# Another deal of three elementwise steps: who rounds and who subtracts the activated sums between two matmuls

## The chip, the cores and the metric

The kernel runs on one core of one Trainium2 chip. A core has five engines, each with its own in-order queue: TensorE (PE; its weight loads are listed apart as PEld), VectorE (DVE), ScalarE (ACT), GpSimd (POOL) and SyncE (SP, which here only issues DMAs). An instruction that waits for a semaphore holds up everything behind it on its own engine. The metric is the device time of one launch in microseconds (us), lower is better; it is given as the median of three runs, and one further execution was taken with the hardware profiler.

## The reference, cut to what matters

Eight batches of eight heads of causal attention (576 positions, head size 64), mixed with a retrieval from a small memory matrix, give a token matrix x of 4608 rows by 512 columns. A feed-forward network follows:

```python
def _moe_ref(x, w_in, w_out):          # x: 4608 x 512
    h = x @ w_in                       # 512 x 2048
    g = h * (1.0 / (1.0 + np.exp(-h))) # h * sigmoid(h)
    return (g @ w_out).astype(np.float32)
```

The kernel writes h * sigmoid(h) as 0.5 * h * (1 + tanh(h / 2)) and applies the 0.5 to the output. To keep the accuracy of 32 bits out of matmuls that round their operands, every operand is held as an upper part (the value rounded to the type `fp32r`) and a lower part (the value less its upper part), and each product is three matmuls: upper by upper, upper by lower, lower by upper.

## The kernel before, in words

Two generators are interleaved. `attention` goes through the 64 heads: one iteration computes the scores of one head and the values of the head before it. `ffn` goes through 18 units of 256 tokens. A unit is 8 steps p; each step makes two 128-row chunks of h in one PSUM bank (24 matmuls, L552), activates them, and multiplies the activated sums g by two chunks of `w_out` into the unit's output banks `acc` (12 matmuls, L532). In the program's text the multiplication of step p-1 stands between the matmuls of step p and the activation of step p, so that PE has work while the activation of a step is under way.

The activation of a step is a chain over three engines: tanh on ScalarE out of PSUM (L563, into the tile `th`), `(th + 1) * h` on VectorE (L564, into `th` again; h is read from PSUM, and when this is done the bank of h is free), the rounding of `th` to the upper part `hi` of the tile `g` on GpSimd (L567), and the subtraction `th - hi` into the lower part `lo` of `g` on VectorE (L568). The matmuls of L532 read `hi` in the first two of each three and `lo` in the third. While attention runs, h has one PSUM bank (`ps_h`); after the last head, odd steps take banks of `ps_t` too. `th` has 4 buffers (tag "row", shared with the output tile), `g` has 4.

The other users of the same engines, as far as the prediction speaks of them: on VectorE the masked scores (L252), the small statistics of a softmax row (`st`: L284 to L302; L290 and L299 read two SBUF tensors), the normaliser (`nrm`: L330 to L333) and the lower parts `pl` and `qp` (L407, L359); on ScalarE the exponentials (L254, L294), and the upper parts `ph` (L406) and `kk`, `qq` (L230, L231, L233); on GpSimd the scaling of the probabilities (L304, five instructions a head, released by L302), the lower parts `kk`, `ql` (L232, L235) and `vs` (L316). L161 and L162 split the weights in the first 200 us: L161 rounds on ScalarE, L162 subtracts on GpSimd, with tiles of the same 128x512 shape as `g`.

The loop at the end of the kernel (L589) decides how many steps of `ffn` follow each step of `attention` (`FFN_RATE`, `FIRST_RATE`). The order of the instructions on each engine is then not the program's: the tile framework is told to schedule with planned costs (`schedule_with_timeline_sim=True`, L631) and moves instructions within what the dependences and buffers allow. A change of engine or operation in one place therefore moves others too.

Of the kernel before, what the change touches and what calls it, by code (L numbers as in the profile page):

```python
# [13 lines left out]
ALU = mybir.AluOpType  # L14
# [26 lines left out]
def memory_attention_then_silu_ffn(ctx, tc, q, k, v, M_prev, z_prev, beta, w_in, w_out, out):  # L41
    nc = tc.nc
# [30 lines left out]
    def f(ap):  # L73
        return ap.bitcast(F32)
# [11 lines left out]
        out=mask[:, 3 * P:], in_=mask[:, 3 * P:], pattern=[[-1, P]], base=0, channel_multiplier=1,  # L86
# [392 lines left out]
    def flow():  # L479
        if flow_order:  # L480
            while flow_order[0] not in ready:
                yield "prepare"
            x = flow_order.pop(0)
            t = weight_tile(*x)
            nc.sync.dma_start(out=f(t), in_=scratch[x])
            flowing.append((x, t))

    def fetch(kind, c):
        if (kind, c) not in FLOW:
            return weight[kind, c]  # L490
        x, t = flowing.pop(0)
        assert x == (kind, c)
        return t

    def split_x(u):
        xu = []
        for kk in range(KD):
            t = pool.tile([P, 2, T], F32R, tag="xu", name="xu", bufs=XU_BUFS)
            t0 = u * T
            while t0 < (u + 1) * T:  # L500
                b = t0 // S
                n = min((b + 1) * S, (u + 1) * T) - t0
                src, o = xt[b, kk][:, t0 - b * S:t0 - b * S + n], t0 - u * T
                nc.scalar.copy(t[:, 0, o:o + n], src)
                nc.vector.tensor_tensor(out=t[:, 1, o:o + n], in0=src, in1=f(t[:, 0, o:o + n]), op=ALU.subtract)  # L505
                t0 += n
            xu.append(t)
        return xu

    def heads_needed(u):  # L510
        return ((u + 1) * T - 1) // S * H + H

    def ffn():
        ahead = None
        for _ in range(FLOW_BUFS):
            yield from flow()
        for u in range(NU):
            while done[0] < heads_needed(u):
                yield "wait"
            xu = ahead or split_x(u)  # L520
            ahead = None
            bank, tag = (ps_s, "s") if done[0] == B * H and u % 2 else (ps_a, "a")
            acc = [bank.tile([P, DM], F32, tag=tag, name="acc") for _ in range(T // P)]

            def second(p, g):
                for c in range(2):
                    w = fetch("o", 2 * p + c)
                    for t in range(T // P):
                        at = slice(t * P, (t + 1) * P)
                        terms = [(g[:, gi, c, at], w[:, wi]) for gi, wi in ((0, 0), (0, 1), (1, 0))]  # L530
                        for n, (ta, tb) in enumerate(terms):
                            nc.tensor.matmul(  # L532
                                acc[t], ta, tb, start=p == 0 and c == 0 and n == 0,
                                stop=p == NP - 1 and c == 1 and n == len(terms) - 1)
                    if ("o", 2 * p + c) in FLOW:
                        yield from flow()

            before = None
            for p in range(NP):
                while not {("i", 2 * p), ("i", 2 * p + 1)} <= ready:  # L540
                    yield "prepare"
                if done[0] == B * H and p % 2:
                    h = ps_t.tile([P, 2, T], F32, tag="t", name="h")
                else:
                    h = ps_h.tile([P, 2, T], F32, tag="h", name="h")
                for c in range(2):
                    w = fetch("i", 2 * p + c)
                    w4 = w.rearrange("p a (k f) -> p a k f", f=P)
                    for kk in range(KD):
                        terms = [(w4[:, wi, kk], xu[kk][:, xi]) for wi, xi in ((0, 0), (0, 1), (1, 0))]  # L550
                        for n, (ta, tb) in enumerate(terms):
                            nc.tensor.matmul(  # L552
                                h[:, c], ta, tb, start=kk == 0 and n == 0,
                                stop=kk == KD - 1 and n == len(terms) - 1)
                    if ("i", 2 * p + c) in FLOW:
                        yield from flow()
                yield
                if before:
                    yield from second(*before)

                h = h.rearrange("p c t -> p (c t)")
                th = pool.tile([P, 2 * T], F32, tag="row", name="th", bufs=ROW_BUFS)
                nc.scalar.activation(th, h, AF.Tanh, scale=0.5)  # L563
                nc.vector.scalar_tensor_tensor(out=th, in0=th, scalar=1.0, in1=h, op0=ALU.add, op1=ALU.mult)  # L564
                g = pool.tile([P, 2, 2, T], F32R, tag="g", name="g", bufs=G_BUFS)
                hi, lo = (g[:, j].rearrange("p c t -> p (c t)") for j in range(2))
                nc.gpsimd.tensor_scalar(hi, th, 1.0, 1.0, op0=ALU.mult, op1=ALU.mult)  # L567
                nc.vector.tensor_tensor(out=lo, in0=th, in1=f(hi), op=ALU.subtract)  # L568
                while not {("o", 2 * p), ("o", 2 * p + 1)} <= ready:
                    yield "prepare"  # L570
                before = p, g
                if p == NP - 2 and u + 1 < NU and done[0] >= heads_needed(u + 1):
                    ahead = split_x(u + 1)
                yield
            yield from second(*before)
            for t in range(T // P):
                o = pool.tile([P, DM], F32, tag="row", name="o", bufs=ROW_BUFS)
                nc.scalar.activation(o, acc[t], AF.Copy, scale=0.5)
                r0 = u * T + t * P
                nc.sync.dma_start(out=out[r0:r0 + P, :], in_=o)  # L580
            yield

    A_STEPS, F_STEPS = 9, 2 * NP + 1
    att, prep, prod = attention(), preparation(), ffn()
    steps, produced, steps_made = 0, 0.0, 0
    going = True
# [46 lines left out]
```

## Time and profile before

| what | value |
|---|---|
| three runs, median (lowest to highest) | 1333.85 us (1330.49 to 1334.98) |
| the profiled execution, its own time / span of its instructions | 1331.87 us / 1330.1 us |
| mean granted TensorE clock | 0.978 |
| busy share of the span | PE 95%, PEld 82%, DVE 72%, ACT 61%, POOL 60% |
| of the chain that ended last | PE 71%, DVE 13%, ACT 6%, DMA 4%, issue 3%, POOL 2% |

In the profile a row names the line of the kernel, the engine, the operation, the tile written and the tiles read, the shape and the count; then busy time in us, the mean ns of one, and the idle time of the engine ahead of it with what ended that idle time. In rows of one tile or one line the three durations are the smallest, the median and the largest. The program has three stages: until about 178 us only attention and the splitting of the weights run, from there to about 1120 us attention and the feed-forward network run together, and from 1120 us to the end only the feed-forward network is left. The first instruction that the change concerns starts at 178.7 us.

### The profile page before, as it was taken

The page shows a single profiled execution, that of the slowest core. Times are in us where ns is not written, and L with a number is a line of the kernel's source. Part 1 is how long each engine was busy: PE and PEld are TensorE (multiplying, and loading weights), DVE is VectorE, ACT ScalarE, POOL GpSimd, SP SyncE. Part 2 cuts the span into 40 slices and gives each one's busy share as a digit, 9 for nine tenths or more (in the row PEclk, how much of TensorE's full clock was granted, in tenths as well). Part 3 has the DMA queues.
Part 4 walks back from the last instruction along what each step waited for, and adds up shares of the span by engine and source line. Part 5 has one row for each costly group of instructions (what it writes and reads, how often), then busy time and mean ns, then how long its engine had stood idle before and what let it go on. Part 6 is the DMA issues. An engine that isn't in the chain of part 4 may idle for free.

```text
span 1330.1 us, 24649 instructions
## 1 busy us (share of the span) xinstructions
PE 1269.9 (95%) x7858; PEld 1084.7 (82%) x7858; DVE 963.4 (72%) x2580; ACT 805.2 (61%) x1999; POOL 798.1 (60%) x1169
## 2 busy tenths in 40 slices
PE   6988989999999999999999999999999999999998
PEld 2343458898989899899989898989898889899997
DVE  7988985788888878877888787778878875322222
ACT  6777765667676767667776676666767663111111
POOL 6888994676666667766677665656576653101110
PEclk9986799999999999999999999999999999999999
DMA  6766555554555545555555455455545432444444
GB/s 163 191 177 176 151 152 159 136 140 134 135 150 137 151 116 135 152 137 151 136 149 140 136 139 136 131 149 136 137 134 145 128 101 80 155 137 155 156 159 143
DMA packets 302994, 190.39 MB, mean 143 GB/s; under 512 B 258832, under 2 KB 267024, under 8 KB 302864
## 3 DMA queue, kind: packets, MB, share of 16 engines
q1 hardware_dynamic: 302864, 188.82, 50.8%
q8 instruction: 62, 1.02, 0.3%
q14 instruction: 68, 0.56, 0.1%
HBM read 173.02 MB, written 15.73 MB: 142 GB/s over the span
## 4 chain that ended last, share of the span: by engine, by line
PE 71%; DVE 13%; ACT 6%; DMA 4%; issue 3%; POOL 2%; SPq 1%; DVEq 0%; POOLq 0%; ACTq 0%
PE h L552 27%; PE acc L532 24%; PE x L422 7%; PE s L250 5%; PE tp L376 4%; DVE s L252 2%; PE x L414 1%; PE tq L351 1%; DMA zb<-in_z_prev 1%; DVE xu L505 1%; DMA flow<-wo_s 1%; DVE th L564 1%; DVE wy L152 1%; DVE wy L159 1%; ACT p L254 1%
## 5 line engine op out<-in xcount | busy, mean ns | idle before, releaser
L552 PE MATMUL h<-xu,wi 128*128 128x256 f32 x2592 | 373.8, 287 | 10.0 <-DVE th L564 7.3
L552 PEld LDWEIGHTS h<-xu,wi 128*128 128x128 f32 x2592 | 342.6, 191 | 24.9 <-DVE th L564 5.9
L304 POOL TENSOR_SCALAR p<-p,st 128x384 f32<-128x384 f32 (+3 forms) x320 | 186.1, 600 | 127.4 <-DVE st L302 121.2
L532 PE MATMUL acc<-wo,g 128*128 128x512 f32 x864 | 244.8, 399 | 0.0
L567 POOL TENSOR_SCALAR g<-th 128x512 fp32r<-128x512 f32 x144 | 90.9, 631 | 236.8 <-DVE th L564 205.7
L532 PE MATMUL acc<-flow,g 128*128 128x512 f32 x864 | 230.9, 395 | 0.7 <-DMA flow<-wo_s 0.7
L254 ACT ACTIVATE p<-s,st 128x128 f32<-128x128 f32 (+3 forms) x256 | 134.9, 528 | 123.2 <-DVE st L252 93.7
L564 DVE SCALAR_TENSOR_TENSOR th<-th,h 128x512 f32<-128x512 f32 x144 | 98.5, 685 | 130.5 <-ACT th L563 128.0
L532 PEld LDWEIGHTS acc<-flow,g 128*128 128x128 f32 x864 | 158.9, 188 | 33.9 <-DMA flow<-wo_s 1.8
L532 PEld LDWEIGHTS acc<-wo,g 128*128 128x128 f32 x864 | 150.0, 189 | 20.1 <-POOL p L304 0.5
L563 ACT ACTIVATE th<-h 128x512 f32<-128x512 f32 x144 | 85.6, 595 | 128.1 <-PE h L552 127.3
L407 DVE TENSOR_TENSOR pl<-tp,ph 128x384 fp32r<-128x384 f32 x216 | 118.4, 550 | 38.1 <-ACT ph L406 33.9
L568 DVE TENSOR_TENSOR g<-th,g 128x512 fp32r<-128x512 f32 x144 | 104.8, 728 | 50.5 <-POOL g L567 49.3
L252 DVE CUSTOM_DVE_ANT_0 s<-s,mask 128x128 f32<-128x128 f32 (+3 forms) x256 | 125.4, 492 | 11.5 <-PE s L250 6.7
L376 PE MATMUL tp<-ident,p 128*128 128x128 f32 x640 | 123.0, 292 | 8.5 <-DVE qp L359 3.7
L552 PE MATMUL h<-xu,flow 128*128 128x256 f32 x864 | 126.7, 284 | 0.0
L406 ACT CAST ph<-tp 128x384 fp32r<-128x384 f32 x216 | 104.7, 490 | 23.6 <-PE x L422 14.7
L552 PEld LDWEIGHTS h<-xu,flow 128*128 128x128 f32 x864 | 114.1, 190 | 0.9 <-issue 0.3
L376 PEld LDWEIGHTS tp<-ident,p 128*128 128x128 f32 x640 | 81.5, 147 | 37.4 <-POOL p L304 9.3
L235 POOL TENSOR_TENSOR ql<-tt,qq 64x512 fp32r<-64x512 f32 x54 | 73.2, 1356 | 20.6 <-ACT qq L231 11.3
L328 POOL TENSOR_TENSOR r<-e,zb 128x320 f32<-128x320 f32 x64 | 59.8, 935 | 42.4 <-DVE e L327 35.4
L422 PE MATMUL x<-pl,vs 128*128 128x256 f32 x324 | 81.7, 307 | 0.0
(103 smaller groups left out, 2430.2 us busy)
## 6 DMA issues: line engine op xcount, KB each, us to landing
flow<-wo_s SPq DMA_DIRECT2D x144, 512.0 KB, 3.5
flow<-wi_s SPq DMA_DIRECT2D x72, 512.0 KB, 3.8
raw<-in_k SPq DMA_DIRECT2D x128, 72.0 KB, 2.3
raw<-in_q SPq DMA_DIRECT2D x128, 72.0 KB, 2.5
out<-o SPq DMA_DIRECT2D x36, 256.0 KB, 4.2
wraw<-in_moe_w_in SPq DMA_DIRECT2D x16, 512.0 KB, 4.4
qn<-in_q SPq DMA_DIRECT2D x64, 128.0 KB, 2.9
vr<-in_v SPq DMA_DIRECT2D x64, 128.0 KB, 2.6
```

What stands on the lines that cost most here:

```text
L252: anchor["dve"] = nc.vector.tensor_tensor_reduce(s, s, mask[:, 3 * P - P * i:], QS, 3.0e38, ALU.add, ALU.min, st[:, i:i + 1]).ins
L254: nc.scalar.activation(pt, s, AF.Exp, bias=st[:, i:i + 1], scale=-1.0, accum_out=st[:, 10 + i:11 + i])
L304: nc.gpsimd.tensor_scalar(pb[x], pb[x], st[:, 15 + x:16 + x], 1.0, op0=ALU.mult, op1=ALU.mult)
L376: nc.tensor.transpose(t[:, o:o + P], pb[i][:, P * j:P * j + P], ident)
L406: nc.scalar.copy(ph[:, 0:o], t[:, 0:o])
L407: nc.vector.tensor_tensor(out=pl[:, 0:cut], in0=t[:, 0:cut], in1=f(ph[:, 0:cut]), op=ALU.subtract)
L422: nc.tensor.matmul(x[0:rows, q0:n], vs[0:n_k, j], part[0:n_k, o:o + n - q0], start=False, stop=last)
L532: nc.tensor.matmul(acc[t], ta, tb, start=p == 0 and c == 0 and n == 0, stop=p == NP - 1 and c == 1 and n == len(terms) - 1)
L552: nc.tensor.matmul(h[:, c], ta, tb, start=kk == 0 and n == 0, stop=kk == KD - 1 and n == len(terms) - 1)
L564: nc.vector.scalar_tensor_tensor(out=th, in0=th, scalar=1.0, in1=h, op0=ALU.add, op1=ALU.mult)
L567: nc.gpsimd.tensor_scalar(hi, th, 1.0, 1.0, op0=ALU.mult, op1=ALU.mult)
L568: nc.vector.tensor_tensor(out=lo, in0=th, in1=f(hi), op=ALU.subtract)
```

## The change

The product of tanh and h stays on VectorE. The rounding to `hi` goes from GpSimd (a multiplication by 1.0 twice) to ScalarE (a copy), and the subtraction for `lo` goes from VectorE to GpSimd. Line numbers do not shift.

```diff
                 nc.vector.scalar_tensor_tensor(out=th, in0=th, scalar=1.0, in1=h, op0=ALU.add, op1=ALU.mult)
                 g = pool.tile([P, 2, 2, T], F32R, tag="g", name="g", bufs=G_BUFS)
                 hi, lo = (g[:, j].rearrange("p c t -> p (c t)") for j in range(2))
-                nc.gpsimd.tensor_scalar(hi, th, 1.0, 1.0, op0=ALU.mult, op1=ALU.mult)
-                nc.vector.tensor_tensor(out=lo, in0=th, in1=f(hi), op=ALU.subtract)
+                nc.scalar.copy(hi, th)
+                nc.gpsimd.tensor_tensor(out=lo, in0=th, in1=f(hi), op=ALU.subtract)
                 while not {("o", 2 * p), ("o", 2 * p + 1)} <= ready:
                     yield "prepare"
```

The order on all engines is the same up to the first step of the feed-forward network, and differs from there on. Three places show how.

On ScalarE, about the middle of the kernel (a tanh and what follows it, among the work of the heads with the tiles `qq_150` and `qq_151`), before:

```order
L275 COPY pair<-s 64x256
L231 CAST qq_151<-tt 64x576
L233 CAST qq_151<-tt 64x576
L563 ACTIVATE th<-h 128x512
L358 CAST qp<-tq 64x2x128
L275 COPY pair<-s 64x320
L230 CAST kk<-tt 64x576
L237 CAST qq_151<-qq_151 128x64
L326 ACTIVATE r<-qn_147 128x320
```

and with the change:

```order
L563 ACTIVATE th<-h 128x512
L275 COPY pair<-s 64x256
L231 CAST qq_151<-tt 64x576
L233 CAST qq_151<-tt 64x576
L358 CAST qp<-tq 64x2x128
L326 ACTIVATE r<-qn_147 128x320
L567 CAST g<-th 128x512
L275 COPY pair<-s 64x320
L230 CAST kk<-tt 64x576
```

The copy (L567) stands five rows behind its tanh here, and the tanh itself moved ahead of the copies of `pair` and `qq`. Over all 144 steps the copy stands directly behind its tanh or with up to seven rows between.

On GpSimd, at the same head, from the end of one head's scaling of the probabilities on, before:

```order
L307 COPY p_6214<-p_6214 64x64
L235 TENSOR_TENSOR ql_154<-tt,qq_150 64x512
L235 TENSOR_TENSOR qq_150<-tt,qq_150 64x64
L318 TENSOR_SCALAR ms<-mr 128x64
L567 TENSOR_SCALAR g<-th 128x512
L319 TENSOR_TENSOR ms<-mr,ms 128x64
L277 TENSOR_TENSOR pair<-pair,mask 64x64
L328 TENSOR_TENSOR r<-e,zb 128x320
```

and with the change:

```order
L307 COPY p_6214<-p_6214 64x64
L318 TENSOR_SCALAR ms<-mr 128x64
L319 TENSOR_TENSOR ms<-mr,ms 128x64
L568 TENSOR_TENSOR g<-th,g 128x512
L328 TENSOR_TENSOR r<-e,zb 128x320
L235 TENSOR_TENSOR ql_154<-tt,qq_150 64x512
L235 TENSOR_TENSOR qq_150<-tt,qq_150 64x64
L277 TENSOR_TENSOR pair<-pair,mask 64x64
```

The subtraction stands where the rounding stood, give or take a few rows, and `ql` has gone behind it.

On PE, the last rows of the program (the matmuls of the last steps; `wo_142` and `wo_144` are the first of the two `w_out` chunks of the last two steps, `flow` is a chunk that is fetched anew), before:

```order
L532 MATMUL acc<-wo_142,g 128x512 x4
L552 MATMUL h<-xu,flow 128x256 x12
L532 MATMUL acc<-wo_142,g 128x512 x2
L532 MATMUL acc<-flow,g 128x512 x6
L532 MATMUL acc<-wo_144,g 128x512 x6
L532 MATMUL acc<-flow,g 128x512 x6
```

and with the change:

```order
L532 MATMUL acc<-wo_142,g 128x512 x6
L552 MATMUL h<-xu,flow 128x256 x12
L532 MATMUL acc<-flow,g 128x512 x6
L532 MATMUL acc<-wo_144,g 128x512 x6
L532 MATMUL acc<-flow,g 128x512 x6
```

Between the last matmul of h and the first that reads the last `g`, eight matmuls stood before, and six stand now.

## The prediction

> **What bounds the kernel now.** I read the busy time by stage first, then PE's own waits in the long middle stage, then the instructions of the tiles `th` and `g`. The first row holds the stage in which attention and the feed-forward network run together, the second the stage with the network alone (columns: stretch, its length, busy us and count of each engine, granted clock, DMA share, GB/s).
>
> ```profile
> 250.00:1120.00 870.00, 847.02 (x5702) 775.04 (x5701) 702.48 (x1993) 596.02 (x1505) 577.97 (x914) 1.00 0.50 136
> 1120.00:1330.00 210.00, 205.35 (x1306) 185.80 (x1304) 58.47 (x98) 34.09 (x69) 23.86 (x37) 1.00 0.44 146
> ```
>
> PE is busy for 847.02 of 870 us (97%) at the full clock, and for 205.35 of the last 210. VectorE is the next at 81%, ScalarE has 69%, GpSimd 66%. The change takes nothing from PE, so in the middle it can touch only the 870 - 847 = 23 us in which PE stands, and these PE names completely:
>
> ```profile
> PE h L552 <- DVE th L564: 6.5, 10, 1.6
> PE tp L376 <- DVE qp L359: 3.7, 2, 2.9
> PE s L250 <- ACT p L254: 3.6, 4, 2.3
> PE s L250 <- DVE st L284: 2.0, 2, 1.0
> PE s L274 <- ACT p L254: 1.8, 2, 1.2
> PE tp L376 <- DVE pl L407: 1.5, 4, 0.5
> PE x L422 <- ACT ph L406: 1.1, 2, 0.5
> PE x L414 <- DVE xt L430: 0.8, 1, 0.8
> PE tq L351 <- DVE ph L410: 0.7, 1, 0.7
> PE h L552 <- DVE st L290: 0.5, 1, 0.5
> PE tq L351 <- ACT th L563: 0.2, 1, 0.2
> PE acc L532 <- DMA flow<-wo_s: 0.2, 1, 0.2
> ```
>
> (Who waited, for whom, us in total, times, longest.) VectorE ends 15.7 us of these waits, ScalarE 6.7, GpSimd none. The largest, 6.5 us, is the one bank of h, which is free when L564 has read it. No matmul of `acc` waits for `g`: neither L567 nor L568 sets PE's time today. What the two cost is room on their engines. VectorE is also whom the others wait for:
>
> ```profile
> ACT p L254 <- DVE st L252: 83.8, 87, 3.0
> ACT p L294 <- DVE st L291: 47.3, 34, 3.2
> POOL p L304 <- DVE st L302: 115.5, 46, 6.4
> POOL g L567 <- DVE th L564: 23.8, 21, 3.4
> DVE g L568 <- POOL g L567: 22.4, 25, 1.8
> ```
>
> **The change part by part, in the middle stage.** It holds 100 of the 144 steps. Their durations, and those of the nearest rows for the two new instructions (the splitting of the weights, the same shape and types, on the engines to which the work goes):
>
> ```profile
> L567 POOL TENSOR_SCALAR g<-th x100: 611/622/729, 257.4 to 1113.6; 128x512 fp32r<-128x512 f32 x100
> L568 DVE TENSOR_TENSOR g<-th,g x100: 645/692/1356, 258.1 to 1114.3; 128x512 fp32r<-128x512 f32 x100
> L564 DVE SCALAR_TENSOR_TENSOR th<-th,h x101: 648/687/691, 256.7 to 1119.6; 128x512 f32<-128x512 f32 x101
> L161 ACT CAST wi<-wy x12: 601/618/652, 12.6 to 155.5; 128x512 fp32r<-128x512 f32 x12
> L162 POOL TENSOR_TENSOR wi<-wy,wi x12: 1264/1278/1725, 13.3 to 161.5; 128x512 fp32r<-128x512 f32 x12
> L568 DVE TENSOR_TENSOR g<-th,g 128x512 fp32r<-128x512 f32 x100 | 72.6, 726 | 23.4 <-POOL g L567 22.4
> ```
>
> *VectorE* loses 72.6 us of work, and the 22.4 us for which it stood in front of L568 for the rounding. Its load goes from 702 to 630 us of 870.
>
> *ScalarE* gains 100 x 0.618 = 62 us: 596 to 658. It also gains a wait that GpSimd had: for L564. GpSimd stood 23.8 us for it in 21 of the 100 steps. With the order shown, from no to seven rows stand between tanh and copy. I bound this idle time by 0 and by one L564 of 0.687 us a step, 69 us, and take 25, by the row of the wait that it replaces. Behind the copy on ScalarE stand the exponentials and the upper parts that PE's transposes and value matmuls need.
>
> *GpSimd* loses 100 x 0.622 = 62 us and gains 100 x 1.278 = 128, or 173 if every one took the longest, 1.725: 578 to 644 us, at most 689. No work of GpSimd is waited for by PE in the list above. The load of the three helpers becomes 73%, 76% and 74%, where the fullest was at 81%.
>
> Not all of VectorE's 95 us stay free. Its small operations with two SBUF inputs are slow against a copy of the same size:
>
> ```profile
> L290 DVE TENSOR_TENSOR st<-st 64x1 f32<-64x1 f32 x102 | 32.0, 313 | 1.1
> L331 DVE SCALAR_TENSOR_TENSOR nrm<-nrm,over 128x5 f32<-128x5 f32 x50 | 25.6, 511 | 1.1
> L299 DVE SCALAR_TENSOR_TENSOR st<-st,over 128x5 f32<-128x5 f32 x52 | 10.2, 196 | 1.1
> L289 DVE COPY st<-st 64x1 f32<-64x1 f32 x102 | 15.2, 149 | 7.2 <-ACT p L294 3.9
> L290 DVE TENSOR_TENSOR st<-st x128: 107/151/1387, 20.4 to 1109.1; 64x1 f32<-64x1 f32 x128
> ```
>
> Over the 149 ns of the copy they lose (313 - 149) x 102 + (511 - 149) x 50 + (196 - 149) x 52 ns = 37 us, and a subtraction of one column that took 1387 ns lasted about as long as a GpSimd subtraction. If they stand behind whatever GpSimd runs, the loss grows with its share and the square of the lengths: a step's 0.62 squared (0.39) becomes 1.28 squared (1.63), two steps a head, against about 9 us squared a head for the rest of GpSimd's work (an estimate from its rows). That is a quarter more, +9 us on VectorE, +37 at the most if the loss doubled. Even then VectorE ends below its load of before.
>
> The Trainium skill, "SBUF — State Buffer", section "Who interferes with whom", states it as a lock: a VectorE instruction with two SBUF inputs and a GpSimd instruction that reads SBUF exclude each other for the whole instruction. The 1387 ns row agrees. The rule speaks against longer GpSimd subtractions, and for taking L568 off VectorE, since L568 itself reads two SBUF tensors; L564 reads one and is not held (its largest duration is 691 ns, its median 687). By that rule at its hardest, the loss doubled to +37 us, VectorE would stand at 77%, its idle time would grow by a fifth and not a third, and the sum at the end would be +1.6 us (1335.5) instead of the one below.
>
> What of this reaches PE: VectorE ends 15.7 us of PE's waits, and its own load falls from 81% to (630 + 9) / 870 = 73%. The waits lie between 0 and 15.7 us shorter; I take the share by which idle time on VectorE grows, 231 from 168 us, a good third: **-6 us**. ScalarE ends 6.7 us; with its idle time down from 274 to 212 - 25 = 187 us, a third less, these grow by half, **+3** (between 0 and +10). New is the lower part: the chain from h to `lo` gets longer by 1.278 - 0.692 = 0.59 us and a wait in another queue. One tight step of the middle:
>
> ```profile
> 600.97 0.59 ACT L563 ACTIVATE th<-h 128x512 f32<-128x512 f32 x1
> 601.59 0.69 DVE L564 SCALAR_TENSOR_TENSOR th<-th,h 128x512 f32<-128x512 f32 x1
> 602.78 0.63 POOL L567 TENSOR_SCALAR g<-th 128x512 fp32r<-128x512 f32 x1
> 604.01 0.67 DVE L568 TENSOR_TENSOR g<-th,g 128x512 fp32r<-128x512 f32 x1
> 605.82 0.86 PE L532 MATMUL acc<-wo,g 128*128 128x512 f32 x3
> ```
>
> `lo` is there at 604.68 and its first reader, the third matmul, starts at about 605.82 + 2 x 0.23 = 606.28 (six such matmuls follow each other in 1.38 us below): 1.6 us to spare, against 0.59 us and one more GpSimd instruction in front at worst (L232, 1.4 us). I put **+1** us for the few steps that miss; the bounds are 0 and +20 (the second rival).
>
> **The last stage.** PE is full, and the three helpers stand most of the time, so the copy takes about the time that the rounding took and only `lo` is later. That shows at the end alone:
>
> ```profile
> 1320.66 0.60 ACT L563 ACTIVATE th<-h 128x512 f32<-128x512 f32 x1 [4.50 <-PE h L552]
> 1322.14 0.62 POOL L567 TENSOR_SCALAR g<-th 128x512 fp32r<-128x512 f32 x1 [4.48 <-DVE th L564]
> 1322.79 0.69 DVE L568 TENSOR_TENSOR g<-th,g 128x512 fp32r<-128x512 f32 x1 [0.81 <-POOL g L567]
> 1322.99 1.54 PE L532 MATMUL acc<-wo,g 128*128 128x512 f32 x6
> 1324.37 1.54 PE L532 MATMUL acc<-flow,g 128*128 128x512 f32 x6
> ```
>
> The third matmul of the last step starts at 1322.99 + 0.46 = 1323.45, just as `lo` is ready (1323.48). With the change `hi` is ready at 1322.76 as now and `lo` at 1322.79 + 1.28 = 1324.07: **+0.6** us. That six matmuls and not eight fill the time before only moves where PE stands.
>
> The sum: -6 + 3 + 1 + 0.6 = -1.4 us. The profiled execution took 1331.87 us, of which 1330.1 are span; it would take 1330.5. The median of the three runs lies 2.0 us above it, so I predict 1333.85 - 1.4, rounded **1332.5 us**. The stretch from 178 to 250 us, with 12 or so steps, I cost at nothing: GpSimd is full of the weights' subtractions there, but the heads' work, not the network, sets that stretch; if that cover is gone, each step's 0.59 us comes to 7 us.
>
> **The rivals.** (1) *VectorE's relief is worth all that it can be.* For it: the rows in which ScalarE stood 83.8 and 47.3 us and GpSimd 115.5 us for VectorE; a shorter queue there speeds the chains on which the heads depend, so that 10 to 15.7 us of PE's 23 go and ScalarE's waits do not grow. Against it: the same stage loads ScalarE by 62 us. Time 1333.85 - 15.7 + 1 = 1319 at the full price, 1325 at a little over half.
>
> (2) *The lower part comes too late* and matmuls of `acc`, which never wait for `g` today, begin to. Place: L568 in GpSimd's queue behind other subtractions. In the tight step above 1.6 us are to spare; 0.59 us longer and one L232-sized instruction in front (I take the 1.278 us of L162) make 1.87 us, and ScalarE's copy may be a row late too (0.6). One step in three late by 0.3 to 0.9 us is 33 x 0.6 = 20 us: 1354; one in five, 1346. It decides from the point where the late steps together cost more than VectorE's waits give back (6 us, ten late steps). Against it: the median step has more room than the tight one shown, and the order on PE leaves six or more matmuls of 0.23 us in between even at the end.
>
> (3) *ScalarE's queue is held by the copy.* At the tight places the copy stands one or two rows behind its tanh, and VectorE reaches L564 late. With the full 69 us of waiting ScalarE has 274 - 62 - 69 = 143 us idle, half of before, and its 6.7 us of PE's waits double or treble: +7 to +13, less the 6 of VectorE. With the probabilities behind it late too, 1340.
>
> **How the numbers follow.** About 0.3%, 4 us, is what a measurement of this kernel can tell from no change, so "same" reaches from 1329.9 to 1337.9. My forecast has 0.40 (its own range 1328 to 1338), rival 1 has 0.32, rival 2 has 0.18, rival 3 has 0.10. Rival 1 and a small part of the forecast (0.03) are faster, 0.35; the rest of the forecast is the same, 0.37; rivals 2 and 3 are slower, 0.28. The range goes to the full price of rival 1 with a little under it, and to one late step in five with a little above: 1317 to 1348.
>
> **What would show it.** Right: PE's waits on VectorE in 250 to 1120 us fall from 15.7 to about 10, those on ScalarE rise to about 10, L568 on GpSimd takes 1.27 to 1.45 us and L567 on ScalarE about 0.62, and VectorE's load in the stage is near 73%. The first rival: PE's idle time there falls under 13 us. The second: rows in which `PE acc L532` waits for `POOL g L568`, 10 us or more together. The third: `ACT g L567` waits for `DVE th L564` with 50 us or more. I am wrong at the root if the time moves by more than PE's named waits can explain, for then PE's busy time hides stalls that this reading does not see.

## The result and the profile after

The changed kernel takes 1319.22 us in the median, against 1333.61 us for the kernel before in the same runs: 14.4 us less, a ratio of 0.9892 (95% interval 0.9871 to 0.9912). One of the four executions of the changed kernel took 2386.78 us, for a reason that is not known, and is left out of the ratio, though the median counts it; the other three took 1317.39 to 1320.44 us, 1318.01 in the median. The profiled execution took 1320.44 us with a span of 1318.7 us, 11.4 us under the profiled execution of before.

Where the span went follows from three marks: the first tanh, the last matmul of attention, and the end. The rows of L563 and L422 by line hold the starts of the first and last instruction; first the kernel before, then the changed one:

```profile
L563 ACT ACTIVATE th<-h x144: 576/598/626, 178.7 to 1320.7; 128x512 f32<-128x512 f32 x144
L422 PE MATMUL x<-pl,vs x324: 220/312/521, 220.5 to 1132.3; 128*128 128x320 f32 x108, 128*128 128x256 f32 x54
```

```profile
L563 ACT ACTIVATE th<-h x144: 576/598/623, 181.7 to 1309.5; 128x512 f32<-128x512 f32 x144
L422 PE MATMUL x<-pl,vs x324: 221/313/396, 223.6 to 1118.6; 128*128 128x320 f32 x108, 128*128 128x256 f32 x54
```

The first tanh comes 3.0 us later (178.7 to 181.7), though nothing ahead of it was changed (the first instruction that itself is changed, the rounding, starts at 186.8 us in the kernel before); this mark lies between 177.9 and 184.9 us in the profiled executions below, so it tells nothing. From it to the last matmul of attention the time falls from 953.6 to 936.9 us, **16.7 us less**. The rest, the network alone, grows from 197.8 to 200.1 us. All of the gain is in the middle.

The two kernels between these marks, by engine (columns as in the prediction: stretch, length, busy us and count of PE, PEld, DVE, ACT and POOL, granted clock, DMA share, GB/s), before and after:

```profile
178.70:1132.30 953.60, 929.10 (x6222) 844.00 (x6222) 757.16 (x2136) 641.65 (x1623) 625.41 (x980) 1.00 0.50 137
```

```profile
181.70:1118.60 936.90, 922.93 (x6230) 841.53 (x6229) 690.57 (x2026) 699.24 (x1731) 671.44 (x978) 1.00 0.52 139
```

For the same matmuls, PE's idle time falls from 24.5 to 14.0 us, and its busy time by 6.2 us. A part of these 6.2 us is the clock. In the kernel before, the granted clock falls to 0.50 twice between the marks, for 3.41 us each (463.91 to 467.32 and 870.09 to 873.50 us); in the changed kernel it never does. The rows of the two stretches show it as 0.99 against 1.00, before and then changed:

```profile
400.00:600.00 200.00, 196.53 (x1319) 180.17 (x1318) 162.45 (x467) 139.67 (x354) 137.34 (x215) 0.99 0.51 138
800.00:1000.00 200.00, 194.03 (x1302) 178.00 (x1301) 159.15 (x452) 132.33 (x337) 128.94 (x206) 0.99 0.50 135
```

```profile
400.00:600.00 200.00, 197.50 (x1339) 181.40 (x1338) 154.93 (x449) 153.97 (x383) 146.72 (x215) 1.00 0.54 144
800.00:1000.00 200.00, 197.65 (x1355) 182.54 (x1353) 147.56 (x443) 151.12 (x376) 145.57 (x213) 1.00 0.53 144
```

PE is busy through both of the 3.41 us, so they cost about 1.7 us each, 3.4 us together (an estimate: half of the time at half the clock). Right ahead of each, PE had stood in one of its two longest waits, 2.3 us for L254 and 2.9 us for L359; in the changed kernel's middle its longest wait is 1.0 us. What the other 2.8 us of busy time were is not shown. VectorE lost 67 us of work, ScalarE gained 58, GpSimd 46.

The long middle stage of the changed kernel alone, and PE's waits in it, complete; they answer to the first row and the list in the prediction:

```profile
250.00:1109.00 859.00, 845.69 (x5741) 777.34 (x5740) 643.87 (x1897) 649.94 (x1611) 622.29 (x914) 1.00 0.52 139
```

```profile
PE h L552 <- DVE th L564: 5.8, 10, 1.0
PE s L250 <- ACT p L254: 4.0, 7, 0.9
PE x L422 <- DVE pl L407: 0.9, 2, 0.6
PE x L422 <- POOL vs L316: 0.8, 1, 0.8
PE tp L376 <- DVE pl L407: 0.5, 2, 0.3
PE x L422 <- ACT ph L406: 0.5, 1, 0.5
PE s L274 <- ACT p L254: 0.3, 1, 0.3
```

VectorE ends 7.2 us of them (15.7 before), ScalarE 4.8 (6.7 before), GpSimd 0.8. No matmul of `acc` waits for `g` here. The waits of the helpers for each other, same stretch:

```profile
ACT p L254 <- DVE st L252: 47.0, 59, 2.4
ACT p L294 <- DVE st L291: 31.3, 31, 2.9
ACT g L567 <- DVE th L564: 26.4, 26, 2.3
POOL p L304 <- DVE st L302: 64.8, 45, 3.3
POOL g L568 <- ACT g L567: 42.1, 32, 4.7
```

ScalarE's two large waits for VectorE fell from 83.8 and 47.3 us, GpSimd's from 115.5. The two new instructions, by line:

```profile
L567 ACT CAST g<-th x101: 603/620/641, 260.4 to 1101.6; 128x512 fp32r<-128x512 f32 x101
L568 POOL TENSOR_TENSOR g<-th,g x101: 1275/1294/1542, 261.2 to 1102.5; 128x512 fp32r<-128x512 f32 x101
```

And the last step of the program, from the timeline (start, duration):

```profile
1310.85 0.62 ACT L567 CAST g<-th 128x512 fp32r<-128x512 f32 x1 [0.76 <-DVE th L564]
1311.52 1.20 PE L532 MATMUL acc<-wo,g 128*128 128x512 f32 x4
1311.54 1.29 POOL L568 TENSOR_TENSOR g<-th,g 128x512 fp32r<-128x512 f32 x1 [5.62 <-ACT g L567]
1312.89 0.74 PE L532 MATMUL acc<-wo,g 128*128 128x512 f32 x2 [0.17 <-POOL g L568]
```

Four matmuls run on `hi`, and the fifth waits until `lo` is there at 1312.83.

### The profile page after: what moved, and what is told of

Same layout as the page of the kernel before. It is cut to its first block, busy times and chain, and to the rows that moved or that the text cites. A ratio compares the mean times of both kernels' runs of the same rounds, so it can differ in the third digit from the quotient of the medians.

```text
span 1318.7 us, 24662 instructions
## 1 busy us (share of the span) xinstructions
PE 1272.7 (97%) x7858; PEld 1085.1 (82%) x7858; DVE 873.2 (66%) x2436; ACT 883.9 (67%) x2143; POOL 868.5 (66%) x1169
## 4 chain that ended last, share of the span: by engine, by line
PE 73%; DVE 10%; ACT 6%; DMA 3%; issue 3%; POOL 2%; SPq 1%; POOLq 0%; DVEq 0%; ACTq 0%
PE h L552 27%; PE acc L532 24%; PE x L422 7%; PE s L250 5%; PE tp L376 4%; PE x L414 2%; PE tq L351 1%; DVE pl L407 1%; DVE s L252 1%; DVE th L564 1%; ACT p L254 1%; ACT th L563 1%; PE s L274 1%; DVE st L290 1%; DVE tt L221 1%
## 5 line engine op out<-in xcount | busy, mean ns | idle before, releaser
L552 PE MATMUL h<-xu,wi 128*128 128x256 f32 x2592 | 377.7, 287 | 9.3 <-DVE th L564 7.2
L568 POOL TENSOR_TENSOR g<-th,g 128x512 fp32r<-128x512 f32 x144 | 186.6, 1297 | 203.5 <-ACT g L567 200.2
L304 POOL TENSOR_SCALAR p<-p,st 128x384 f32<-128x384 f32 (+3 forms) x320 | 182.5, 590 | 76.7 <-DVE st L302 73.7
L254 ACT ACTIVATE p<-s,st 128x128 f32<-128x128 f32 (+3 forms) x256 | 134.9, 528 | 70.7 <-DVE st L252 53.5
L563 ACT ACTIVATE th<-h 128x512 f32<-128x512 f32 x144 | 85.9, 597 | 99.2 <-PE h L552 98.7
L552 PE MATMUL h<-xu,flow 128*128 128x256 f32 x864 | 122.4, 283 | 0.0
L567 ACT CAST g<-th 128x512 fp32r<-128x512 f32 x144 | 89.2, 620 | 49.1 <-DVE th L564 48.3
L422 PE MATMUL x<-pl,vs 128*128 128x256 f32 x324 | 82.1, 308 | 1.0 <-DVE pl L407 0.9
L232 POOL TENSOR_TENSOR kk<-tt,kk 64x576 fp32r<-64x576 f32 x54 | 77.3, 1431 | 5.0 <-ACT kk L230 1.2
L235 POOL TENSOR_TENSOR ql<-tt,qq 64x512 fp32r<-64x512 f32 x54 | 69.8, 1293 | 15.1 <-ACT qq L231 6.7
```

What stands on the lines that cost most here:

```text
L254: nc.scalar.activation(pt, s, AF.Exp, bias=st[:, i:i + 1], scale=-1.0, accum_out=st[:, 10 + i:11 + i])
L304: nc.gpsimd.tensor_scalar(pb[x], pb[x], st[:, 15 + x:16 + x], 1.0, op0=ALU.mult, op1=ALU.mult)
L422: nc.tensor.matmul(x[0:rows, q0:n], vs[0:n_k, j], part[0:n_k, o:o + n - q0], start=False, stop=last)
L552: nc.tensor.matmul(h[:, c], ta, tb, start=kk == 0 and n == 0, stop=kk == KD - 1 and n == len(terms) - 1)
L568: nc.gpsimd.tensor_tensor(out=lo, in0=th, in1=f(hi), op=ALU.subtract)
```

## The experiments

Theory Q, formed from these readings: PE pays for the queue on VectorE, and the gain is VectorE's relief. Its rivals: O, luck of the planner's new order; G, the rounding leaving GpSimd; L, fewer operations with two SBUF inputs on VectorE. Each edit below shows the lines at the place of the change alone. The first four runs do half of the change each, or give VectorE its time back.

**Only the rounding moves** (`e1`, on the kernel before):

```diff
-                nc.gpsimd.tensor_scalar(hi, th, 1.0, 1.0, op0=ALU.mult, op1=ALU.mult)
+                nc.scalar.copy(hi, th)
```

> The kernel before with the first half of the change alone: the rounding goes from GpSimd to ScalarE, the subtraction stays on VectorE. VectorE's load in the middle stage stays at about 81%, ScalarE's rises from 596 to about 658 us, GpSimd's falls from 578 to about 516. Theory Q (VectorE's queue is what PE pays for, and its relief brought the 14 us): no gain, 1330 to 1340 us, PE's waits on VectorE stay at 12 us or more. Rival O (the gain is luck of the new order of instructions, whatever the loads): anything between 1318 and 1338. Rival G (the gain comes from the rounding leaving GpSimd, so that the scaling of the probabilities there starts sooner): 1318 to 1324.

Measured: 1336.48 us against 1334.05, ratio 1.0017 (0.9996 to 1.0038): no gain, as theory Q had it. Rival G falls.

**Only the subtraction moves** (`e2`, on the kernel before):

```diff
-                nc.vector.tensor_tensor(out=lo, in0=th, in1=f(hi), op=ALU.subtract)
+                nc.gpsimd.tensor_tensor(out=lo, in0=th, in1=f(hi), op=ALU.subtract)
```

> The kernel before with the second half of the change alone: the subtraction goes from VectorE to GpSimd, the rounding stays on GpSimd. VectorE falls from 702 to about 640 us in the middle stage, ScalarE stays at 596, GpSimd rises from 578 to about 707 of 870 us (81%). Theory Q: most of the gain is there, 1318 to 1326, with PE's waits on VectorE at 10 us or less; what GpSimd's fuller queue costs (scaling of the probabilities later, or matmuls of acc that wait for the subtraction) is the rest. Rival O: anything between 1318 and 1338. Rival G: 1333 or slower, since GpSimd gains 130 us and loses nothing.

Measured: 1349.92 us, ratio 1.0118 (1.0081 to 1.0155), slower by 16 us. VectorE has the relief and the gain isn't there: theory Q as first put falls. The stretch from the first tanh to the last attention matmul, and PE's longest waits in 250 to 1109 us:

```profile
178.10:1144.30 966.20, 935.73 (x6212) 849.81 (x6213) 706.83 (x2027) 642.11 (x1622) 742.01 (x1089) 0.99 0.49 135
```

```profile
PE h L552 <- DVE th L564: 7.2, 10, 2.3
PE x L414 <- DVE xt L430: 4.8, 4, 2.1
PE h L552 <- DVE xu L505: 3.2, 1, 3.2
```

VectorE works 707 us, near the changed kernel's 691, but GpSimd is at 742 of 966. PE waits 1.3 us for GpSimd in this stretch and 24.9 us for VectorE. That VectorE is late because GpSimd is, is argued and not shown: VectorE's own largest waits in 250 to 1109 us are for ScalarE (38.1, 28.5 and 23.7 us), and the chain from there to GpSimd was not followed.

**VectorE's time given back** (`e3` and `e4`, on the changed kernel; in `e3`, `spare` is a tile of one column that is made once):

```diff
                 nc.gpsimd.tensor_tensor(out=lo, in0=th, in1=f(hi), op=ALU.subtract)
+                nc.vector.tensor_reduce(spare, th, axis=AX.X, op=ALU.add)
```

> The changed kernel with VectorE's time given back as idle work: after each subtraction a sum over the 512 columns of th is made on VectorE into a column that nobody reads (one SBUF input, about 0.7 us a step by the rows of the 320-column sum, 0.48 us). VectorE is back at about 81% of the middle stage, everything else is as in the changed kernel. Theory Q: most of the gain is gone, 1328 to 1336, PE's waits on VectorE back at 12 us or more. Rival O: 1317 to 1324 or anywhere, with no tie to VectorE's load. Rival L (the gain comes from taking an operation with two SBUF inputs off VectorE, which held GpSimd and was held by it): stays at 1317 to 1322, since the sum has one input.

```diff
                 nc.gpsimd.tensor_tensor(out=lo, in0=th, in1=f(hi), op=ALU.subtract)
+                spare = pool.tile([P, 2 * T], F32, tag="row", name="spare", bufs=ROW_BUFS)
+                nc.vector.tensor_tensor(out=spare, in0=th, in1=f(hi), op=ALU.subtract)
```

> The changed kernel in which VectorE makes the subtraction too, into a spare tile that nobody reads (two SBUF inputs, and it waits for ScalarE's rounding as it waited for GpSimd's before; the spare tile takes one of the four buffers that th and the output tile share). Theory Q: 1328 to 1338, the same as the run with the sum within 4 us, or a little above it for the waits in front of the subtraction. Rival L: 1333 or more, and well above the run with the sum. Rival O: anywhere between 1317 and 1338.

Measured: 1345.56 us (ratio 1.0104, 1.0063 to 1.0145) with the sum and 1366.45 us (1.0248, 1.0211 to 1.0286) with the second subtraction. The sum alone, with one SBUF input and no reader, takes away 26 us, more than the gain: rival L is not needed for that. Both lie above what theory Q gave; that ScalarE and GpSimd keep their new work is the likely reason, which theory R below takes up. The second subtraction costs 21 us beyond the sum. Its three differences (two SBUF inputs, a wait for the rounding, a buffer of `th`) were not told apart, so what of the 21 us is contention stays open. The stretch of each:

```profile
179.50:1141.70 962.20, 932.34 (x6230) 842.52 (x6229) 760.45 (x2135) 697.40 (x1731) 671.51 (x979) 0.99 0.50 136
```

```profile
182.90:1168.80 985.90, 946.60 (x6226) 853.01 (x6224) 789.05 (x2136) 699.17 (x1731) 714.84 (x980) 0.99 0.48 133
```

**Other orders of the same work** (`e5` to `e8`). A slightly different rate at which the network's steps are dealt makes the planner order the same instructions anew:

```diff
-FFN_RATE = 0.22
+FFN_RATE = 0.219      # e5 on the kernel before, e6 on the changed one
+FFN_RATE = 0.221      # e7 on the kernel before, e8 on the changed one
```

> The kernel before with FFN_RATE 0.219 in place of 0.22: the same instructions, dealt a little later, in another order (about a quarter to all of the rows of each engine's list move). This measures what an order is worth by itself. Theory Q (loads of the helpers decide): 1330 to 1338 us. Rival O (luck of the order): as far from 1334 as the change is, 10 us or more either way.

> The changed kernel with FFN_RATE 0.219. Theory Q: 1315 to 1325 us, still 10 us or more below the kernel before with the same rate. Rival O: up to 1333, and no gap to the kernel before with the same rate.

> The kernel before with FFN_RATE 0.221, another order of the same instructions. Theory Q: 1330 to 1338 us. Rival O: 10 us or more away from 1334.

> The changed kernel with FFN_RATE 0.221. Theory Q: 1315 to 1325 us. Rival O: up to 1333, and no gap to the kernel before with the same rate.

Measured, with the kernel before at 1333.88: `e5` 1334.94 (ratio 1.0007, 0.9986 to 1.0028), `e7` 1335.24 (1.0022, 1.0004 to 1.0041), `e6` 1320.95 (0.9915, 0.9882 to 0.9948), `e8` 1324.06 (0.9927, 0.9899 to 0.9955). The old deal stays within 1.4 us, the new one within 5 us, and a gap of 11 to 14 us remains at each rate. Rival O falls as a cause of the whole gain; an order can be worth some 5 us.

**The other two helpers burdened** (`e9`, `e10`, on the changed kernel). Theory R, formed now: PE pays for whichever of the three is fullest.

```diff
+                nc.gpsimd.tensor_scalar(lo, th, 1.0, 1.0, op0=ALU.mult, op1=ALU.mult)   # e9
                 nc.gpsimd.tensor_tensor(out=lo, in0=th, in1=f(hi), op=ALU.subtract)
```

> The changed kernel with GpSimd burdened: ahead of each subtraction GpSimd writes th, multiplied by 1, into the lower part, which the subtraction then overwrites (the 0.62 us that it spent on the rounding before, to no use). GpSimd goes from 622 to about 685 of the middle stage's 859 us (80%), VectorE and ScalarE have the changed kernel's work. Theory R, formed from the first four runs (PE pays for whichever of the three helpers gets near 80%, not for VectorE alone): 1335 to 1352 us, like the run that moved only the subtraction. Theory Q (VectorE alone): 1318 to 1326.

```diff
                 nc.scalar.copy(hi, th)
+                nc.scalar.copy(hi, th)                                                  # e10
```

> The changed kernel with ScalarE burdened: the rounding is made twice, into the same place. ScalarE goes from 650 to about 712 of 859 us (83%), and the lower part is ready 0.62 us later. Theory R: 1335 to 1352 us. Theory Q: 1318 to 1326.

Measured: `e9` 1345.25 us (1.0103, 1.0071 to 1.0134), `e10` 1354.18 us (1.0162, 1.0131 to 1.0193), against 1332.98. Both are far from theory Q; `e9` lies in theory R's range and `e10` 2 us above it. Some 0.62 us a step on either engine costs 26 to 35 us against the changed kernel, as much as on VectorE or more. In `e10` the lower part is also 0.62 us later; PE waited 0.9 us for the rounding by its list of waits, so that is not where the time went. The stretches of `e9` and `e10`:

```profile
180.20:1144.20 964.00, 936.05 (x6226) 846.34 (x6226) 705.67 (x2027) 698.42 (x1731) 740.70 (x1089) 0.99 0.49 136
```

```profile
180.30:1150.20 969.90, 937.50 (x6215) 852.28 (x6215) 700.69 (x2027) 753.19 (x1842) 676.22 (x980) 0.99 0.49 134
```

**VectorE subtracts after the last head** (`e11`) **and in every other step** (`e12`), on the changed kernel:

```diff
+                sub = nc.vector if done[0] == B * H else nc.gpsimd      # e11
+                sub = nc.vector if p % 2 else nc.gpsimd                 # e12
-                nc.gpsimd.tensor_tensor(out=lo, in0=th, in1=f(hi), op=ALU.subtract)
+                sub.tensor_tensor(out=lo, in0=th, in1=f(hi), op=ALU.subtract)
```

> The changed kernel, but after the last head, where the helpers stand most of the time, the subtraction goes back to VectorE (0.69 us instead of 1.29). The middle stage stays as it is. The last stage took 2.3 us longer with the change than before (200.1 against 197.8 us from the last attention matmul on); if the later lower part is the cause, 1 to 2 us come back: 1316 to 1319; if not, 1318 to 1321.

Measured: 1313.76 us, ratio 0.9870 (0.9837 to 0.9903), the fastest of all and below both ranges expected. The last stage, changed kernel first, then `e11`:

```profile
1118.60:1318.70 200.10, 193.56 (x1216) 173.70 (x1214) 29.95 (x54) 53.29 (x99) 45.17 (x35) 1.00 0.45 148
```

```profile
1121.90:1318.30 196.40, 192.05 (x1216) 173.75 (x1214) 54.12 (x89) 53.63 (x99) 0.00 (x0) 1.00 0.44 150
```

The same matmuls take 3.7 us less. The intervals of the two ratios overlap and the two were not timed side by side, so that it beats the change by the whole difference is not shown; that its last stage is shorter is, in the one profiled execution of each.

> The changed kernel with the subtraction of every odd step back on VectorE: VectorE between the two kernels (about 79%), GpSimd at about 69%, ScalarE at 76%. Theory R and theory Q: between the changed kernel and the run that moved only the rounding, 1324 to 1332 us. If the half-way deal is as good as the change or better (1322 or less), the loads are not what decides at this size.

Measured: 1336.09 us, ratio 1.0026 (1.0003 to 1.0050): no gain at all, above both theories' range. Its stretch, and that of `e1` for comparison:

```profile
177.90:1133.10 955.20, 931.15 (x6212) 844.12 (x6212) 718.29 (x2081) 696.71 (x1732) 615.97 (x926) 0.99 0.50 136
```

```profile
178.70:1134.00 955.30, 929.18 (x6214) 843.99 (x6213) 746.86 (x2136) 697.32 (x1731) 560.32 (x871) 0.99 0.50 136
```

Put together, the busy time of the fullest helper between the two marks, the length of the stretch, and the time in it at a granted clock of 0.50, all in us:

```
kernel                       fullest helper   stretch   at clock 0.50
e6, changed, rate 0.219      ScalarE  697      937.0        0
e8, changed, rate 0.221      ScalarE  697      944.2        0
changed                      ScalarE  699      936.9        0
e11                          ScalarE  699      937.0        0
e12                          VectorE  718      955.2       10.2
e9                           GpSimd   741      964.0       10.2
e2                           GpSimd   742      966.2       23.9
e1                           VectorE  747      955.3       10.2
e10                          ScalarE  753      969.9       27.3
before                       VectorE  757      953.6        6.8
e5, before, rate 0.219       VectorE  758      955.6       13.6
e7, before, rate 0.221       VectorE  760      953.7       13.6
e3                           VectorE  760      962.2       10.3
e4                           VectorE  789      985.9       27.3
```

Every deal whose fullest helper works under 700 us is fast, and none above is. But the step between 699 and 718 us holds the whole gain, and from 718 to 760 us the stretch does not grow with the load (953.6 to 969.9 us, in no order). The clock parts the kernels at the same place: the first four never drop to half between the marks, all of the others do. Half of the time in the last column (an estimate of what it costs, as above) is a fifth to two fifths of what each of them takes beyond 936.9 us. So the clock adds to the long waits of PE, and is not the whole of the gain. Theory R thus holds for the sign and not for the size: the half-way deal should have been half-way. The starts of every eighth tanh (L563, in the timeline) show how the two kinds differ; their distances in us, from the 25th to the 105th step:

```
before   70.8 70.5 65.9 68.6 69.6 67.4 72.3 69.0 70.0 71.4
changed  68.2 67.7 67.9 67.6 67.5 67.5 67.6 66.6 67.9 66.4
e12      68.6 71.4 70.4 70.2 69.3 71.3 72.8 69.9 66.8 65.7
```

The changed kernel keeps one pace. The other two have stretches as fast or faster (65.9, 65.7) and others of 70 to 73 in between. What makes these longer ones, the load itself or the order that the planner makes of a deal at that load, is not settled: no run held the order and changed the load.

## Why the prediction was right and wrong

The measured 1319.22 us lies in the range of 1317 to 1348, but it is the time of rival 1 at its full price (1319, with the chance 0.32), not of the forecast of 1332.5 (1328 to 1338), which had 0.40. That it is the full price is luck: VectorE still ends 7.2 us of PE's waits, and PE's idle time in the middle stage is 13.3 us, just above the 13 that was set as the sign of rival 1. The rest came out of PE's busy time, for which rival 1 had no term either.

- *What bounds the kernel.* Right: PE, with 23 us named. 10.5 us of its idle time went between the marks. Not seen: 6.2 us more went out of what the profile counts as busy, which is what I had given as the sign of a wrong root. About 3.4 of them are the two drops of the clock behind PE's longest waits, a cost for which the sum had no term; the rest is open.
- *The durations and loads.* Right: 0.620 and 1.294 us against 0.618 and 1.278; VectorE 644 us of 859 in the middle (forecast 639), ScalarE 650 (658), GpSimd 622 (644). ScalarE's wait in front of the copy, taken as 25 us, was 26.4.
- *The loss of VectorE's small operations with two SBUF inputs*, +9 us. Right: in the changed kernel's rows, below, the mean of L290 is 364 ns and that of L331 478, of L299 276, so (364 - 149) x 103 + (478 - 149) x 50 + (276 - 149) x 52 ns = 45 us, 8 more than the 37. One of the three went the other way: L331 fell from 511 ns.
- *VectorE's waits, -6 us.* Mis-sized: 15.7 to 7.2, -8.5.
- *ScalarE's waits, +3 us.* The step that failed in sign: 6.7 to 4.8, -1.9. I took ScalarE's idle time as slack and let its loss lengthen the queue. But PE's waits for it did not grow, and this does not hang on VectorE's relief: in `e1`, with the copies and VectorE's old work, PE waits 5.4 us for ScalarE. ScalarE's waits for VectorE at L254 and L294, 131 us before and 78 in the changed kernel, are 111 us in `e1` and 128 in `e2`, which has the relief without the copies. So the copies partly fill time in which ScalarE would have waited, and most of the shrinking comes with both halves together; which of them does what is not told apart further. The rows of 83.8 and 47.3 us stood in the prediction, as what speaks for rival 1, and were not used in the sum.
- *The lower part, +1 us in the middle.* No wait for it there. The margin of the tight step was enough, and rivals 2 and 3 did not come, as far as the change itself goes. Rival 2's engine, GpSimd, is nevertheless where a little more work is dear: `e2` and `e9` show it, by PE's waits for VectorE and not by late matmuls of `acc`.
- *The end, +0.6 us.* Mis-sized: the mechanism is there (0.17 us of waiting at the last step), but the last stage grew by 2.3 us, and `e11` took 3.7 out of it.
- *The stretch from 178 to 250 us*, at nothing. The reason given was wrong: GpSimd worked 46.8 of those 72 us, and four of its instructions there are the weights' subtractions. PE itself was busy for 70.5 of the 72 us, and for all of them with the change; no cost shows there.

The rows for ScalarE, in 250 to 1109 us: PE's waits for it in `e1`, then its two waits for VectorE in `e1` and in `e2`:

```profile
PE s L250 <- ACT p L254: 2.1, 2, 1.4
PE s L274 <- ACT p L254: 1.9, 2, 1.2
PE x L414 <- ACT p L254: 1.4, 1, 1.4
```

```profile
ACT p L254 <- DVE st L252: 73.9, 85, 2.4
ACT p L294 <- DVE st L291: 37.0, 35, 2.7
```

```profile
ACT p L254 <- DVE st L252: 80.3, 81, 3.3
ACT p L294 <- DVE st L291: 47.5, 41, 3.1
```

Summed: where I had -6 and +3 us for PE's waits in the middle stage, the rows show -8.5 and -1.9, and +0.8 for GpSimd, together -9.6 us. With the 6.2 us of busy time that is nearly all of the 16.7 us by which the middle became shorter.

## What to carry to other kernels

When three helpers feed one full engine, less idle time on a helper does not mean that its queue grows in proportion: here 62 us of copies on ScalarE left PE's waits for it no longer (6.7 us before, 5.4 in `e1`, 4.8 with the change). Read who ended a helper's idle time before counting work against it. A lower load on the fullest helper is not enough by itself: `e12` lowered it from 757 to 718 us, with the others below, and gained nothing, while the whole move lowered it to 699 and gained 14 us. Either half of the move alone gained nothing or lost 16 us. Try the whole deal and its halves, since they do not add up, and put back on the quick engine what is moved in a stage where the helpers stand idle. Look at the granted clock beside the waits: a long wait of the full engine can cost more than its own length.

## What the runs showed of the hardware

The granted clock fell to 0.50 for 3.41 us or twice that between the marks of each of the ten kernels with a helper above 700 us, and of none of the four without. In the kernel before, PE had worked 1.09 and 1.23 us of the 3.41 us right ahead of the two drops. PE's longest wait between the marks is 1.7 to 3.6 us in the ten and 1.0 to 1.9 us in the four; how much PE has to stand for a drop was not measured.

A VectorE operation of one column with two SBUF inputs takes longer in the kernels in which GpSimd works more. L290 in the middle stage of `e1`, the changed kernel and `e2`, in this order (the kernel before has 313 ns):

```profile
L290 DVE TENSOR_TENSOR st<-st 64x1 f32<-64x1 f32 x103 | 31.3, 304 | 2.0
```

```profile
L290 DVE TENSOR_TENSOR st<-st 64x1 f32<-64x1 f32 x103 | 37.5, 364 | 2.3
L331 DVE SCALAR_TENSOR_TENSOR nrm<-nrm,over 128x5 f32<-128x5 f32 x50 | 23.9, 478 | 1.2
L299 DVE SCALAR_TENSOR_TENSOR st<-st,over 128x5 f32<-128x5 f32 x52 | 14.4, 276 | 1.0
```

```profile
L290 DVE TENSOR_TENSOR st<-st 64x1 f32<-64x1 f32 x99 | 39.4, 398 | 1.4
```

GpSimd works 560, 671 and 742 us between the marks in these three. Over all profiled executions there are two groups and no finer order: the mean of L290 is 277 to 327 ns in the five with GpSimd at 560 to 628 us, and 343 to 433 ns in the nine at 671 us and more. The latter are also those in which GpSimd makes the long subtractions of all steps in the middle, so load and length are not told apart, and L331 shows no such order. That L290 takes longer there agrees with the exclusion that the Trainium skill states ("SBUF — State Buffer", "Who interferes with whom"). The size had been expected. What had not is how dear GpSimd's time is for PE: in `e2` and `e9`, with GpSimd at 742 and 741 us, the stretch is some 10 us longer than with VectorE at 747 and 757 us in `e1` and the kernel before. That the exclusion is the reason for this is not shown.
